# Cross-covariance attention with a gated FFN: norms from running sums, products spread over three chunks, first softmax by blocks, last stores by pairs

## The chip, the cores and the metric

The kernel runs on one core of one Trainium2 chip. The metric is device time in microseconds (us) for one execution: 810.92 us before the change, the median of 3 runs (810.77 to 811.05).

## What is computed

For each of 4 batches, q, k and v have N = 6016 rows and C = 256 columns. The attention is over columns: q and k are divided by the norm of each of their columns, the 256x256 matrix of their products is put through a softmax, and v is multiplied by it. The 24064 rows of the result then pass a gated feed-forward layer of width 1536.

```python
qn = q / (np.linalg.norm(q, axis=1, keepdims=True) + 1e-06)
kn = k / (np.linalg.norm(k, axis=1, keepdims=True) + 1e-06)
s = kn.transpose(0, 2, 1) @ qn / tau
a = np.exp(s - s.max(-1, keepdims=True))
a /= a.sum(-1, keepdims=True) + 1e-09
x = (v @ a).reshape(24064, 256)
gate = 1.0 / (1.0 + np.exp(-(x @ w_gate)))
out = (gate * (x @ w_val)) @ w_out
```

tau is 1. All inputs and the output are float32; the matmuls take bfloat16.

## The kernel before

A batch has 47 row tiles of 128 rows, worked off as 12 chunks (`groups`): eleven of four tiles and one of three. The attention is folded into the feed-forward weights: with e the exponentials, G = e w_gate and H = e w_val, each row divided by its sum of e, are made once a batch, so that a chunk needs only v times G and v times H. G and H come from 12 products (`gh_order`) of two matmuls of 512 columns each.

A chunk has 12 slots, one per block of 128 of the 1536 hidden columns. In a slot `glu` issues two matmuls into `ps_gate` and two into `ps_val`; ScalarE makes a tanh (L516), VectorE combines it with `ps_val` into `hT` (L517). Each of the two PSUM tags has two buffers. The products with w_out belong to the chunk before (`out_work`): per pair of row tiles seven half-size products instead of eight, in Strassen's manner, whose operands VectorE adds up from `hT` (`a_sum`, L539). `run_work` issues in every slot its share of them. When a pair is through, ScalarE copies it out (L593, L600) and GpSimd makes the last additions (L594, L595, L608, L609). SyncE stores whole chunks.

The order of everything is written out by hand: `tc.manual_schedule()` keeps the program's order on each engine. Next to chunks of batch b, `side_work` puts steps for batch n = b+1 at numbered slots, chunk times 12 plus slot. A step is issued at the end of its slot, after `glu`, the sums and the share of output products:

- slots 0 to 95: loads of q and k on GpSimd's queue, two `score` matmuls per row tile, squares by ScalarE and their running sums `acc` in VectorE (`acc_square`, `acc_add`; L278). The last `acc_add` is in slot 96 for batch 1, and in slot 95 for batches 2 and 3.
- slots 97 to 114: `acc_fold`, three steps for q and three for k (L288, L292, L295, L296): four row sums become one in float32, which is split into two bfloat16 parts.
- slot 117: `norms_mm` sums over the partitions with 8 products of one column into `ps_n`. Slot 118: `root_seed` (two VectorE operations) and `root_steps` (13 small GpSimd operations). Slot 124: `norms_inv` (L369, L370). Slot 125: `spread_both` puts k's inverse norms along the columns with float32 matmuls (`ps_rk`). Slot 126: ScalarE copies it. Slot 127: `scale_x` (L308). Slots 128, 129: `exps`. Slot 131: `sums_both`.
- slots 132 to 143: one of the 12 `gh` products each, with alternating PSUM buffers; even ones are evicted by ScalarE (L464), odd ones by VectorE (L466).

Batch 0 has a head of its own: q and k come by DMA in groups (`groups0`), with squares, running sums and scores as they land. `busy` issues idle matmuls between them. Then come a root by ScalarE (`norms_sqrt`), `norms_inv`, copies of the scores (`copy_s`), `spread_k`, `weights` (two products on VectorE per block, then an exponential), the first transposed v, the row sums and four `gh` products; the other eight follow in chunk 0.

The last chunk's output rows have a tail of their own: `end_rows` makes rows 0 and 1 with plain products, `store` stores what is in `stores`, and `last_rows` stores these two rows on SyncE's queue, makes the last row tile in two halves and stores one on SyncE's and one on ScalarE's queue.

## Time and profile before

| what | value |
|---|---|
| median of 3 runs | 810.92 us |
| the profiled execution | 811.63 us |
| its span, first to last instruction | 809.9 us |
| mean granted TensorE clock | 0.997 |
| TensorE busy | 785.4 us (97%) |
| VectorE busy | 719.5 us (89%) |
| ScalarE busy | 525.8 us (65%) |
| GpSimd busy | 351.9 us (43%) |
| first gate product of chunk 0 | 38.03 us |
| last matmul starts | 804.46 us |

Engines in the profile: PE is TensorE's matmul, PEld its weight load, DVE VectorE, ACT ScalarE, POOL GpSimd, SP SyncE; a q behind an engine's name stands for its queue. A timeline line gives the start, the duration, the engine, the line of the kernel, the operation, output<-inputs, the shapes and, in brackets, how long the engine was idle before it and what ended that. Matmuls are pipelined: a product of 512 columns has a duration of 0.38 us, and the next one starts 0.216 us after it. A line of the table of stages gives from:to, the elapsed time, and for each engine its busy time with the number of instructions, then the granted clock, the DMA engines' share and GB/s. Times in a stage count from the start of the span.

### The profile page before, as it was taken

The numbers are of one execution on the slowest core, as the hardware profiler recorded it, in microseconds if no ns is written. First come the engines' busy times: TensorE is split into PE (matmuls) and PEld (weight loads), VectorE is DVE, ScalarE is ACT, GpSimd is POOL, SyncE is SP. The second block draws the span as 40 slices with busy tenths as digits, with TensorE's granted clock in tenths as the row PEclk, the third lists the DMA queues.
The fourth block names the chain that finished last, engine by engine and source line by source line (L and its number), as shares of the span: only waits on it lengthen the run. The fifth ranks groups of instructions, "written<-read, shape, count | busy, mean of one in ns | idle before, by whom it ended". The sixth has DMA issues, their size and how long they took to land.

```text
span 809.9 us, 17873 instructions
## 1 busy us (share of the span) xinstructions
PE 785.4 (97%) x6742; PEld 500.3 (62%) x6754; DVE 719.5 (89%) x1230; ACT 525.8 (65%) x887; POOL 351.9 (43%) x566
## 2 busy tenths in 40 slices
PE   4799999999999999999999999999999999999997
PEld 2556666666666666666666666666666666666665
DVE  5768999999889999999997999999998898998995
ACT  3666777765667777775566677776566566566563
POOL 4572545433543454334543543443353234444343
PEclk9999999999999999999999999999999999999999
DMA  9995757422856557423285477523223433323302
GB/s 214 207 207 96 129 99 139 89 63 47 137 102 122 90 115 126 84 53 78 58 148 105 94 124 111 103 68 78 60 53 74 78 53 80 79 53 85 68 27 74
DMA packets 76775, 78.24 MB, mean 97 GB/s; under 512 B 50704, under 2 KB 54288, under 8 KB 76688
## 3 DMA queue, kind: packets, MB, share of 16 engines
q0 software_dynamic: 21648, 39.59, 29.6%
q1 hardware_dynamic: 54752, 36.91, 20.0%
q8 instruction: 53, 0.87, 0.4%
q10 hardware_dynamic: 288, 0.59, 0.2%
q14 instruction: 34, 0.28, 0.1%
HBM read 78.64 MB, written 24.64 MB: 128 GB/s over the span
## 4 chain that ended last, share of the span: by engine, by line
PE 89%; DVE 5%; DMA 3%; issue 1%; ACT 1%; POOL 0%; POOLq 0%; DVEq 0%
PE ps_gate L127 28%; PE ps_val L127 28%; PE ps_o L127 26%; PE ps_s L127 4%; DMA k_sb<-in_k_dram 3%; DVE hT L517 2%; PE ps_gh L127 2%; DVE sums L539 1%; ACT g_sb L516 1%; DVE fold L295 0%; PE ps_rk L127 0%; DVE two L292 0%; DVE acc L278 0%; POOL q_sb L137 0%; PE ps_end L127 0%
## 5 line engine op out<-in xcount | busy, mean ns | idle before, releaser
L516 ACT ACTIVATE g_sb<-ps_gate 128x512 f32<-128x512 f32 (+1 forms) x576 | 338.3, 588 | 228.5 <-PE ps_gate L127 218.6
L517 DVE SCALAR_TENSOR_TENSOR hT<-g_sb,ps_val 128x512 bf16<-128x512 f32 (+1 forms) x576 | 384.8, 671 | 68.4 <-ACT g_sb L516 59.9
L127 PE MATMUL ps_val<-vT,gh_H 128*128 128x512 bf16 (+1 forms) x1152 | 337.5, 375 | 2.0 <-DVE hT L517 2.0
L127 PE MATMUL ps_gate<-vT,gh_G 128*128 128x512 bf16 (+1 forms) x1152 | 337.5, 375 | 0.4
L539 DVE TENSOR_TENSOR sums<-hT 128x768 bf16<-128x768 bf16 (+1 forms) x460 | 280.4, 610 | 0.0
L127 PEld LDWEIGHTS <-sums 128*128 128x128 bf16 x2670 | 183.1, 98 | 82.2
L127 PEld LDWEIGHTS <-gh_H 128*128 128x128 bf16 x1152 | 112.7, 98 | 133.6 <-issue 3.4
L608 POOL TENSOR_TENSOR out_sb<-out_sb,m_sb 128x256 f32<-128x256 f32 x89 | 76.8, 863 | 244.7 <-ACT out_sb L600 216.2
L127 PE MATMUL ps_o<-w_sums,sums 128*128 128x128 bf16 x1602 | 154.7, 219 | 0.0
L127 PEld LDWEIGHTS <-hT 128*128 128x128 bf16 x1200 | 88.3, 98 | 46.7
L594 POOL TENSOR_TENSOR m_sb<-m_sb 128x128 f32<-128x128 f32 x89 | 41.7, 469 | 155.4 <-ACT m_sb L593 155.3
L127 PEld LDWEIGHTS <-gh_G 128*128 128x128 bf16 x1152 | 96.9, 98 | 15.1 <-DVE gh_G L466 0.5
L127 PE MATMUL ps_o<-w_out_sb,sums 128*128 128x128 bf16 x1068 | 96.2, 219 | 0.0
L127 PE MATMUL ps_o<-w_sums,hT 128*128 128x128 bf16 x1068 | 95.7, 219 | 0.0
L127 PE MATMUL ps_s<-k_sb,q_sb 128*128 128x256 bf16 x376 | 71.4, 293 | 14.5 <-DMA k_sb<-in_k_dram 7.6
L609 POOL TENSOR_TENSOR out_sb<-out_sb 128x256 f32<-128x256 f32 x89 | 77.7, 873 | 7.0
L600 ACT COPY out_sb<-ps_o 128x512 f32<-128x512 f32 x89 | 52.2, 586 | 14.3 <-PE ps_o L127 11.6
L278 DVE TENSOR_TENSOR acc<-acc,sq 128x1024 bf16<-128x1024 bf16 (+1 forms) x66 | 59.8, 906 | 0.0
L595 POOL TENSOR_TENSOR m_sb<-m_sb 128x128 f32<-128x128 f32 x89 | 53.5, 601 | 7.0
L240 ACT ACTIVATE sq<-k_sb 128x1024 bf16<-128x1024 bf16 (+2 forms) x44 | 44.8, 1027 | 11.9 <-DMA k_sb<-in_k_dram 11.9
L127 PEld LDWEIGHTS <-q_sb 128*128 128x128 bf16 x376 | 33.8, 105 | 20.0 <-issue 8.9
L593 ACT COPY m_sb<-ps_o 128x384 f32<-128x384 f32 x89 | 42.7, 479 | 2.6 <-PE ps_o L127 0.3
(82 smaller groups left out, 313.3 us busy)
## 6 DMA issues: line engine op xcount, KB each, us to landing
out_dram<-out_sb SPq DMA_DIRECT2D x44, 512.0 KB, 3.4
v_sb<-in_v_dram POOLq DMA_DIRECT2D x44, 256.0 KB, 5.2
q_sb<-in_q_dram POOLq DMA_DIRECT2D x35, 256.0 KB, 4.4
k_sb<-in_k_dram POOLq DMA_DIRECT2D x35, 256.0 KB, 5.7
q_sb<-in_q_dram POOLq DMA_DIRECT2D x4, 512.0 KB, 11.5
k_sb<-in_k_dram POOLq DMA_DIRECT2D x4, 512.0 KB, 13.4
w_f<-in_moe_w_out_dram POOLq DMA_DIRECT2D x3, 512.0 KB, 10.5
out_dram<-out_sb SPq DMA_DIRECT2D x3, 384.0 KB, 2.8
```

Of the source, the lines that this page charges most:

```text
L127: nc.tensor.matmul(out, lhsT=lhsT, rhs=rhs, start=start, stop=stop, **kw)
L240: nc.scalar.activation(out=sq[:, :nt, :], in_=src[:, :nt, :], func=ACT.Square)
L278: nc.vector.tensor_tensor(out=acc[:, :nt, :], in0=acc[:, :nt, :], in1=st[b]["sq", w][:, :nt, :], op=ALU.add)
L516: nc.scalar.activation(out=g_sb[:, :n], in_=ps_gate[:, :n], func=ACT.Tanh, scale=0.5)
L517: nc.vector.scalar_tensor_tensor(out=hts[b, ci][:, f, :n], in0=g_sb[:, :n], scalar=1.0, in1=ps_val[:, :n], op0=ALU.add, op1=ALU.mult,)
L539: nc.vector.tensor_tensor(out=sums[b, ci, g][:, m, :, : half * P], in0=hT[:, f0 + k0 : f1 : 2, ds(r0 * half * P, half * P)], in1=hT[:, f0 ...
L593: nc.scalar.copy(m, states[p]["ps"][:, : 3 * P].rearrange("p (n c) -> p n c", c=P))
L594: nc.gpsimd.tensor_tensor(out=m[:, 1, :], in0=m[:, 1, :], in1=m[:, 2, :], op=ALU.add)
L595: nc.gpsimd.tensor_tensor(out=m[:, 2, :], in0=m[:, 1, :], in1=m[:, 0, :], op=ALU.add)
L600: nc.scalar.copy(o[:, p : p + half + 1 : half, :], states[p]["ps"].rearrange("p (t c) -> p t c", c=C),)
L608: nc.gpsimd.tensor_tensor(out=ends, in0=ends, in1=states[p]["m"][:, 1:3, :], op=ALU.add)
L609: nc.gpsimd.tensor_tensor(out=ends, in0=ends, in1=mids, op=ALU.subtract)
```

## The change

The fold is gone: `norms_mm` takes the products of the four running sums themselves, 16 instead of 8. All steps from `norms_mm` on move ahead: `norms_mm` to slot 97, `root_seed` and `root_steps` to 98, `norms_inv` to 106, `spread_both` to 107, the copy to 108, `scale_x` to 109 and 110, `exps` to 111 and 112, the row sums to 114. The 12 `gh` products go to slots 116, 118, 121, 123, 126, 128, 131, 133, 136, 138, 141 and 143.

In the head, the last group's scores are issued before the last norm products, the copies of the scores before `norms_inv`, and four short `busy` products become two `busy_long` of float32 after groups 6 and 8; later ones are fewer. `weights` multiplies a block with k's inverse norms in one VectorE operation, and q's go into the exponential as its scale, one ScalarE operation for each 128 columns. The row sums (`row_sums`, for `sums_both`) are made block by block, VectorE alone evicts the first transposed v, and the `gh` evictions change engines.

In the tail, chunk 10 of the last batch is stored by pairs of rows, each when its additions are done; those of its last pair are made by VectorE instead of GpSimd. Its output products are shared over 11 slots of the last chunk instead of 12. Each of the rows of `end_rows` is stored at once on ScalarE's queue.

```diff
--- before.py
+++ after.py
@@ -279,27 +279,10 @@
             out=acc[:, :nt, :], in0=acc[:, :nt, :], in1=st[b]["sq", w][:, :nt, :], op=ALU.add
         )
 
-    def acc_fold(b, w, step):
-
-        s = st[b]
-        if step == 0:
-            acc = s["acc"][w]
-            s["two"] = attp.tile([P, 2, C], FP32, tag="two", name="two")
-            nc.vector.tensor_tensor(out=s["two"], in0=acc[:, :2, :], in1=acc[:, 2:, :], op=ALU.add)
-            return
-        one, other = s["two"][:, 0, :], s["two"][:, 1, :]
-        if step == 1:
-            nc.vector.tensor_tensor(out=one, in0=one, in1=other, op=ALU.add)
-            return
-        fold = attp.tile([P, 2, C], BF16, tag=f"fold{w}", name="fold")
-        nc.vector.tensor_copy(out=fold[:, 0, :], in_=one)
-        nc.vector.tensor_tensor(out=fold[:, 1, :], in0=one, in1=fold[:, 0, :], op=ALU.subtract)
-        s.setdefault("fold", []).append(fold)
-
     def norms_mm(b):
         s = st[b]
         s["n"] = psm.tile([P, 2 * CB], FP32, tag="m", name="ps_n")
-        norm_mms(s["n"], s["fold"], 2, True, True)
+        norm_mms(s["n"], s["acc"], TPC, True, True)
 
     def scale_x(b, j):
         s = st[b]
@@ -391,18 +374,17 @@
         s = st[b]
         e = attp.tile([P, CB, P], BF16, tag=f"e{i}", name=f"e_sb{i}", bufs=2)
         y = attp.tile([P, CB, P], FP32, tag=f"y{i}", name="y_sb")
+        nc.vector.tensor_tensor(
+            out=y,
+            in0=s["x"][:, :, ds(i * P, P)],
+            in1=s["rk"][i].rearrange("p (o c) -> p o c", o=1).to_broadcast([P, CB, P]),
+            op=ALU.mult,
+        )
         for j in range(CB):
-            nc.vector.scalar_tensor_tensor(
-                out=y[:, j, :],
-                in0=s["x"][:, j, ds(i * P, P)],
-                scalar=s["r"][:, j : j + 1],
-                in1=s["rk"][i],
-                op0=ALU.mult,
-                op1=ALU.mult,
-            )
-        nc.scalar.activation(out=e, in_=y, func=ACT.Exp, bias=shift)
+            nc.scalar.activation(
+                out=e[:, j, :], in_=y[:, j, :], func=ACT.Exp, bias=shift, scale=s["r"][:, j : j + 1]
+            )
         s.setdefault("e", []).append(e)
-        s.setdefault("rrow", [])
 
     def exps(b, i):
 
@@ -412,26 +394,27 @@
             out=e, in_=s["x"][:, :, ds(i * P, P)], func=ACT.Exp, bias=shift
         )
         s.setdefault("e", []).append(e)
-        s.setdefault("rrow", [])
-
-    def sums_both(b):
-        s = st[b]
-        ps_r = psm.tile([P, CB], FP32, tag="m", name="ps_r")
-        for i in range(CB):
+
+    def row_sums(b, i0, ni, pl, tag):
+        s = st[b]
+        ps_r = pl.tile([P, ni], FP32, tag=tag, name="ps_r")
+        for i in range(ni):
             for j in range(CB):
                 mm(
                     ps_r[:, i : i + 1],
-                    s["e"][i][:, j, :],
+                    s["e"][i0 + i][:, j, :],
                     ones_bf[:, 0:1],
                     start=(i == 0 and j == 0),
                     stop=(j == CB - 1),
                     skip_group_check=True,
                 )
-        r = attp.tile([P, CB], FP32, tag="rrow", name="rrow", bufs=2)
+        r = attp.tile([P, ni], FP32, tag=f"rrow{i0}", name="rrow", bufs=2)
+        half = attp.tile([P, ni], FP32, tag=f"rhalf{i0}", name="rhalf", bufs=2)
         invert(r, ps_r, 1e-9, 1.0)
-        half = attp.tile([P, CB], FP32, tag="rhalf", name="rhalf", bufs=2)
         nc.vector.tensor_scalar(out=half, in0=r, scalar1=0.5, scalar2=None, op0=ALU.mult)
-        s["rrow"] = [[x[:, i : i + 1] for i in range(CB)] for x in (r, half)]
+        rrow = s.setdefault("rrow", ([], []))
+        for x, to in zip((r, half), rrow):
+            to.extend(x[:, i : i + 1] for i in range(ni))
 
     def gh_tiles(b):
         st[b]["gh"] = [
@@ -605,9 +588,14 @@
             c00, c11 = 2 * p, 2 * (half + p) + 1
             ends = blocks[:, c00 : c11 + 1 : c11 - c00, :]
             mids = blocks[:, c00 + 1 : c11 : max(1, c11 - c00 - 2), :]
-            nc.gpsimd.tensor_tensor(out=ends, in0=ends, in1=states[p]["m"][:, 1:3, :], op=ALU.add)
-            nc.gpsimd.tensor_tensor(out=ends, in0=ends, in1=mids, op=ALU.subtract)
-            if p == half - 1:
+            last = (b, ci) == (B - 1, NCH - 2)
+            add = (nc.vector if last and p == half - 1 else nc.gpsimd).tensor_tensor
+            add(out=ends, in0=ends, in1=states[p]["m"][:, 1:3, :], op=ALU.add)
+            add(out=ends, in0=ends, in1=mids, op=ALU.subtract)
+            if last:
+                t0 = groups[ci][0]
+                nc.sync.dma_start(out=out_rows[b][:, t0 + p : t0 + nt : half, :], in_=o[:, p:nt:half, :])
+            elif p == half - 1:
                 stores.append((b, ci))
 
         def single(s, f):
@@ -652,14 +640,15 @@
         ps = pso.tile([P, CH], FP32, tag="o", name="ps_o")
         for f in range(FC):
             mm(ps[:, :C], hT[:, f, ds(s * P, P)], w_out_sb[:, f, :], f == 0, f == FC - 1)
-        nc.vector.tensor_copy(out=out_tile(b, ci)[:, s, :], in_=ps[:, :C])
+        o = out_tile(b, ci)[:, s, :]
+        nc.vector.tensor_copy(out=o, in_=ps[:, :C])
+        nc.scalar.dma_start(out=out_rows[b][:, groups[ci][0] + s, :], in_=o)
 
     def last_rows(b, ci):
 
         t0, nt = groups[ci]
         s, half = nt - 1, C // 2
         hT = hts[b, ci]
-        nc.sync.dma_start(out=out_rows[b][:, t0 : t0 + s, :], in_=ffn[b, ci][:, :s, :])
         for n, queue in enumerate((nc.sync, nc.scalar)):
             ps = pso.tile([P, half], FP32, tag="o", name="ps_end")
             for f in range(FC):
@@ -674,6 +663,11 @@
         ps = psg.tile([P, CH], FP32, tag="g", name="ps_busy")
         for _ in range(n):
             mm(ps, ones_bf, ones_wide, True, True)
+
+    def busy_long():
+
+        ps = psg.tile([P, CH], FP32, tag="g", name="ps_busy")
+        mm(ps, ident_f, ident_f.rearrange("p (o c) -> p o c", o=1).to_broadcast([P, TPC, P]), True, True)
 
     ps_n0 = psm.tile([P, 2 * CB], FP32, tag="m", name="ps_n")
 
@@ -702,37 +696,34 @@
             ends.append((sq, nt))
         if g == last0:
             norm_mms(ps_n0, acc, TPC, True, False)
+        for u in range(nt):
+            score(0, t0, u)
+        if g == last0:
             for n, (end, rows_n) in enumerate(ends):
                 norm_mms(ps_n0, end, rows_n, False, n == len(ends) - 1, (1, 0) if n else (0, 1))
-        for u in range(nt):
-            score(0, t0, u)
-        if n_acc - 4 <= g < n_acc:
-            busy(1)
+        if g in (6, 8):
+            busy_long()
     st[0]["n"] = ps_n0
     norms_sqrt(0)
     nc.scalar.preload_act_table(ACT.Exp)
-    norms_inv(0)
     copy_s(0, 0)
     copy_s(0, 1)
-    busy(3)
+    norms_inv(0)
+    busy(2)
     spread_k(0, 0, pso, "o")
     spread_k(0, 1, pso, "o")
-    busy(1)
     weights(0, 0)
     weights(0, 1)
-    late = []
-    transpose_v(
-        0, 0, psv.tile([P, TPC * CB, P], BF16, tag="v", name="ps_tp"), lambda *a: late.append(a)
-    )
-    nc.scalar.copy(*late.pop())
+    transpose_v(0, 0, psv.tile([P, TPC * CB, P], BF16, tag="v", name="ps_tp"))
     gh_tiles(0)
 
-    ps_first = gh_mms(0, 0, psg, "g")
-    sums_both(0)
-    gh_store(0, 0, ps_first, False)
-    gh(0, 1, psg, "g", act=True)
-    gh(0, 2, psv, "v", act=False)
-    gh(0, 3, psv, "v", act=True)
+    row_sums(0, 0, 1, psm, "m")
+    gh(0, 0, psg, "g", act=True)
+    row_sums(0, 1, 1, pso, "o")
+    gh(0, 1, psg, "g", act=False)
+    gh(0, 2, psv, "v", act=True)
+    gh(0, 3, psv, "v", act=False)
+
 
     def side_work(b):
 
@@ -776,23 +767,21 @@
         if n + 1 < B:
             for g, (t0, nt) in enumerate(groups[:3]):
                 at(NCH * FC - 24 + 8 * g, load_qk, n + 1, t0, nt)
-        for i in range(6):
-            at(8 * FC + 1 + (7 * i + 1) // 2, acc_fold, n, *divmod(i, 3))
-        s0 = 10 * FC - 3
+        s0 = 8 * FC + 1
         at(s0, norms_mm, n)
         at(s0 + 1, root_seed, n)
         at(s0 + 1, root_steps, n)
-        at(s0 + 7, norms_inv, n)
-        at(s0 + 8, spread_both, n)
-        at(s0 + 9, copy_rk, n)
-        at(s0 + 10, scale_x, n, 0)
-        at(s0 + 10, scale_x, n, 1)
-        at(s0 + 11, exps, n, 0)
-        at(s0 + 12, exps, n, 1)
-        at(s0 + 14, sums_both, n)
-        at(s0 + 14, gh_tiles, n)
+        at(s0 + 9, norms_inv, n)
+        at(s0 + 10, spread_both, n)
+        at(s0 + 11, copy_rk, n)
+        at(s0 + 12, scale_x, n, 0)
+        at(s0 + 13, scale_x, n, 1)
+        at(s0 + 14, exps, n, 0)
+        at(s0 + 15, exps, n, 1)
+        at(s0 + 17, row_sums, n, 0, CB, psm, "m")
+        at(s0 + 17, gh_tiles, n)
         for i in range(len(gh_order)):
-            at(s0 + 15 + i, gh, n, i, *((pss, "s"), (psm, "m"))[i % 2])
+            at(s0 + 19 + 5 * i // 2, gh, n, i, *((pss, "s"), (psm, "m"))[i % 2])
         return side
 
 
@@ -812,7 +801,7 @@
                         store()
                     if f + final in NEXT_SLOTS and prev != (0, 0):
                         a_sum(*prev, 1, NEXT_SLOTS[f + final])
-                    run_work(work, 1 / (FC - f))
+                    run_work(work, 1 / max(1, FC - final - f))
                 if f in OWN_SLOTS and not final and (b, ci) != (0, 0):
                     a_sum(b, ci, 0, OWN_SLOTS[f])
                 for fn, a in side.get((ci, f), ()):
```

## The prediction

> **What bounds the kernel now.** I read the page first, then the table of stages, then TensorE's and VectorE's timelines where a stage is longer than its neighbours, then the head and the tail.
>
> From the page: busy time, and the chain that ended last.
>
> ```profile
> PE 785.4 (97%) x6742; PEld 500.3 (62%) x6754; DVE 719.5 (89%) x1230; ACT 525.8 (65%) x887; POOL 351.9 (43%) x566
> PE 89%; DVE 5%; DMA 3%; issue 1%; ACT 1%; POOL 0%; POOLq 0%; DVEq 0%
> ```
>
> TensorE sets the pace; the 5% DVE in the chain are the places where something else does. The table of stages, one line per chunk: a clean chunk of the last batch, then chunks 8 to 11 of the second (elapsed, then busy time of PE, weight loads, DVE, ACT, POOL).
>
> ```profile
> 742.90:757.96 15.06, 15.06 (x137) 9.40 (x134) 13.60 (x23) 9.14 (x16) 6.28 (x9) 1.00 0.32 71
> 363.89:379.68 15.79, 15.21 (x136) 9.38 (x134) 15.75 (x26) 9.14 (x16) 6.17 (x9) 1.00 0.31 69
> 379.68:394.93 15.25, 15.25 (x144) 9.58 (x142) 15.06 (x28) 9.15 (x16) 5.97 (x9) 1.00 0.27 62
> 394.93:411.11 16.18, 15.86 (x143) 10.01 (x141) 14.21 (x29) 10.09 (x19) 9.88 (x24) 1.00 0.55 98
> 411.11:428.78 17.67, 17.51 (x160) 11.73 (x160) 15.25 (x32) 11.38 (x23) 7.98 (x13) 1.00 0.64 120
> ```
>
> A clean chunk has no TensorE idle, so one slot (one `glu` call with its share of output products) is 15.05/12 = 1.254 us. Chunk 8 is 0.74 longer without more TensorE work, and its DVE is full (15.75 of 15.79). Chunk 11 holds all twelve G and H products: 24 matmuls of 0.216 are 5.18, a three-row chunk is 12.45 (the last of the kernel), the sum 17.63 against 17.67. So the products are not stalled where they are. The two stalls in the timelines of batch 0 (VectorE, then TensorE):
>
> ```profile
> 181.37 1.01 DVE L539 TENSOR_TENSOR sums<-hT 128x768 bf16<-128x768 bf16 x1
> 182.31 0.81 DVE L295 CAST fold<-two 128x256 bf16<-128x256 f32 x1
> 183.15 0.43 DVE L296 TENSOR_TENSOR fold<-two,fold 128x256 bf16<-128x256 f32 x1
> 183.49 0.68 DVE L517 SCALAR_TENSOR_TENSOR hT<-g_sb,ps_val 128x512 bf16<-128x512 f32 x1
> ...
> 183.05 0.59 PE L127 MATMUL ps_gate<-vT,gh_G 128*128 128x512 bf16 x2
> 184.22 0.59 PE L127 MATMUL ps_val<-vT,gh_H 128*128 128x512 bf16 x2 [0.58 <-DVE hT L517]
> 185.04 0.59 PE L127 MATMUL ps_gate<-vT,gh_G 128*128 128x512 bf16 x2
> ...
> 207.49 0.50 PE L127 MATMUL ps_o<-w_out_sb,sums 128*128 128x128 bf16 x6
> 208.36 0.71 PE L127 MATMUL ps_rk<-ident_f,r 128*128 128x128 f32 x4 [0.38 <-DVE r L370]
> ```
>
> The fold makes a gate product late, and TensorE, two buffers ahead, waits: the slot is 1.99 long, 0.74 too long. Then `ps_rk` starts 0.54 late, because `norms_inv` is queued on DVE one slot before it. Both recur in batches 1 and 2 (0.74 and 0.75; 0.49 and 0.62). Some single gaps of 0.219 before products of `ps_gh` are missing records: 38 of the 48 `w_gate` products are in the trace. The tail, SyncE's timeline:
>
> ```profile
> 802.96 0.33 SPq L647 DMA_DIRECT2D out_dram<-out_sb  x1
> 803.82 0.33 SPq L662 DMA_DIRECT2D out_dram<-out_sb  x1
> 804.36 1.52 SPq L669 DMA_DIRECT2D out_dram<-end  x1
> ```
>
> 512, 256 and 64 KB go out within 1.4 us. The two `end` transfers land 4.1 us (SyncE) and 3.3 us (ScalarE, issued at 805.03) after issue, at 808.50 and 808.33; 1.36 us of closing semaphores follow to 809.86.
>
> **What the Trainium skill says.** "TensorE: Matmul & The Clock Gate", *What's actually happening*: after an idle window of about 3.4 us the array runs at half rate until it has been busy for about as long. The trace agrees: products of 256 columns are 0.109 apart at 26.4, 0.213 from 26.7 to 29.7, 0.109 from 30.35. "DMA: Bandwidth & Descriptors", *Anatomy of one DMA*: about 2.0 us fixed plus bytes/436 GB/s; the 384 KB stores give 2.9 by it, 2.8 here. "GPSIMD Engine Reference", *Key points*: GpSimd shares its SBUF interfaces with VectorE when that reads two SBUF inputs; here the same `sums` operation takes 0.55 alone and 1.01 beside L608/L609.
>
> **The change part by part** (us, minus is gain).
>
> *Folds gone.* Six DVE operations a batch, by their rows 2x(0.68+0.67+0.55+0.43) = 4.7 of DVE time. What they cost the end is only the stall: 0.74+0.74+0.75 = -2.23. All else of them lay beside TensorE.
>
> *Norm products on `acc` itself.* 16 instead of 8, at 0.0255 apart (chunk 9's excess of 0.204 over 8): +0.20 a batch, +0.61. Their place is now slot 97, one slot after the last `acc_add` in batch 0 (slot 96), two in batches 1 and 2 (slot 95). In the trace of before that add ends 0.56 after slot 98 begins in batch 0, and 0.35 before it in the others. The first eight products (of q's sums) take 0.20, so the rest wait about 0.41 in batch 0 and nothing else: +0.41. Queued behind them are the gate products of slot 98, which have no other way.
>
> *`root_seed`, `root_steps`, `norms_inv`, `spread_both` earlier.* The 13 GpSimd steps took 4.1 (200.80 to 204.87); ahead of them on POOL is only chunk 7's last addition, and DVE asks for `r` eight slots (10 us) later: hidden. `spread_both` still comes one slot after `norms_inv`. At slot 106 with DVE not late: gate at 376.43 in batch 1, tanh ends at +1.23, hT 0.60, the slot's `sums` 0.47, inverse to first product 0.42 (as at 207.94 to 208.36): 379.21, while TensorE is there at 376.43+2.51 = 378.94. Stall 0.27, against 0.54, 0.49, 0.62: -0.83 over three batches. Bounds: DVE free of waits and no stall, -1.65; as before, 0.
>
> *Products spread.* The same 24 matmuls, evictions and weight loads in slots 116 to 143; nothing was stalled, so 0. The cover is DVE's slack in chunk 9: 15.05-13.60 = 1.45, plus TensorE's new work there 0.10+2x0.43 = 0.96, against DVE's new work 2x0.48 (`scale_x`) + 0.73 (row sums inverted) + 0.74 (one eviction) = 2.43. That just balances, and a gate product may be 1.08 late before TensorE feels it (hT ends 1.86 after its slot's start; the product that reuses its buffer starts at 2.94). Bounds: 0, and all DVE evictions in the four-row slots exposed, which the rivals use.
>
> *Head.* DMA lands the last of k at 32.31 and the first gate weights at 35.91 either way. Moving two score products ahead of the last norm products delays the root 33.04 to 33.19 and brings the copies of s to 32.92 to 33.64; `norms_inv` behind them ends at 33.93 (before 33.63). `ps_rk` to first use 0.64: 34.57. Two DVE operations of 128x256 (0.42, 0.34 apart; L387 takes 0.41, L308 0.48) replace four of 0.34. Four exponentials of 128 columns with two pointer operands: by "ScalarE: Activation LUTs", *What ACT_TABLE_LOAD costs*, 0.186+2x0.093+0.107 = 0.48 each, 0.39 apart, an estimate (the page gives 0.49 for the old form, the trace 0.507). First block ready at 35.90, second at 36.67, instead of 35.42 and 35.94. The first product stays at 36.05, held by its weights; the second waits until 36.80 (before 36.58). Evictions then end at 37.41, 38.19, 38.55, 39.05, and the first gate products run at 38.09 instead of 38.03: +0.06. The late block uses up slack that evictions had. `busy_long` is four `ps_rk`-like products (2x0.112 each), 0.9 warm and 1.8 cold: the second ends at about 29.3, and groups 9 and 10 are through by 31.4, before the k of group 11 lands at 31.61. The dropped and changed `busy` products stand against the clock gate: between 33.4 and 36.8 TensorE would be busy 57% instead of 72%; between 19.8 and 23.2 it was about 55% and the clock held. Bounds: -0.15; +2.0 if the clock falls for one window (half of 3.4, and the late block).
>
> *Tail.* With the output work done in 11 slots, 7.64 products go into a slot instead of 7; slots of 1.042 become 1.078 and slot 10 ends at 799.90. The last pair's two additions go to DVE before the last hT: ScalarE's copy ends at 800.70, two additions of 0.42 (L296's 0.43) to 801.55, hT to 802.05, while row 0's twelfth product wants it at 801.76: TensorE +0.35. In return 256 KB leave at about 799, 256 at 801.6, 128 at 802.9 and 804.2, and the last 64 KB at 805.38 (805.03+0.35) with little ahead. The new issues on ScalarE's queue (0.35 each) have no other work beside them. Fixed part and size give 2.15; I take 2.4 for what still overlaps: lands 807.8 instead of 808.5, so -0.7. Bounds -1.2 (2.0, no stall) and +0.3 (3.3 again).
>
> Sum: -2.23+0.61+0.41-0.83+0.06-0.7 = -2.68. The profiled execution took 811.63, of which 809.86 span and 1.8 around it; it would take 808.95. It lies 0.7 above the median of the runs, 810.92, so the median becomes 808.2.
>
> **The rivals.** *The waits only move* (same): `norms_mm`, `spread_both` and the last hT all wait on DVE by one slot. If `spread_both` gains nothing (+0.83), each batch waits for `acc` (+0.8) and the tail is even (+0.7), 2.3 come back: 810.5. For it, the 0.54 before; against it, the 0.35 margin in batches 1 and 2. *DVE becomes the bound in chunks 9 and 10* (slower): four evictions of 0.74 a batch fall into full slots. If POOL's sharing stretches the operations there, as it did the fold's cast (0.81 against 0.28), and their time shows in full, 4x0.74-1.08 = 1.9 a batch, 5.6 in all: 813.8. It ends on the slow side once over 1.4 a batch shows. For it, the balance of chunk 9; against it, chunk 11, which takes six such evictions without a stall. *More than forecast*: no stall at `ps_rk`, no wait in batch 0, tail -1.2: 806.4. *The clock falls in the head*: +1.9, 810.1, belongs to "same".
>
> **How the numbers follow.** Forecast 0.54 (own range 807.0 to 809.3, by the bounds of head, tail and `ps_rk`); waits move or clock falls 0.24; DVE bound 0.17; more 0.05. 0.2% (1.6 us, about what a measurement of this kernel can tell from no change) puts nearly all of the first case and the last into faster: 0.58; same 0.24; slower 0.18. The range 806.6 to 812.6 leaves out the upper part of the DVE case and a little below.
>
> **What would show it.** Right: no slot of 1.99 at 107; a gap of about 0.4 before `ps_n` in batch 0 alone; `ps_rk` 0.2 to 0.3 late; first gate products within 0.3 of 38.0; last landing about 2.4 after the last issue. Wrong: TensorE waiting for DVE's hT or evictions in chunks 9 or 10, products of 0.43 instead of 0.216 after 36, a last transfer that lands 3 us or more after issue.

## The result and the profile after

The changed kernel takes 808.53 us (median of 6 runs, 808.16 to 808.78) against 811.03 (6 runs of the kernel before, 810.77 to 811.05): a ratio of 0.9969, 95% interval 0.9957 to 0.9982. The forecast was 808.2, range 806.6 to 812.6. The profiled execution took 808.34 us, its span 806.5 (806.48 unrounded) against 809.86: 3.38 less. Read part by part, those 3.38 us come from three places, and one of them, the last chunk with the stores behind it, gave more than twice what was predicted:

| place | before | after | difference | predicted |
|---|---|---|---|---|
| start to the first gate product of chunk 0 | 38.03 | 38.18 | +0.16 | +0.06 |
| chunks 8 to 11, batch 0 | 64.95 | 64.62 | -0.33 | |
| the same, batch 1 | 64.89 | 64.19 | -0.70 | |
| the same, batch 2 | 65.03 | 64.19 | -0.84 | |
| sum of these three | | | -1.87 | -2.04 |
| first gate product of the last chunk to the end | 21.80 | 20.14 | -1.67 | -0.7 |
| span | 809.86 | 806.48 | -3.38 | -2.68 |

Each column is one profiled execution. That of the kernel before (811.63) lies above all six of its timed runs, and the median moved by 2.50 us, less than the span.

The page of the changed kernel, engines' busy time and the chain that ended last:

```profile
PE 785.5 (97%) x6776; PEld 500.1 (62%) x6776; DVE 707.7 (88%) x1209; ACT 526.4 (65%) x888; POOL 356.7 (44%) x564
PE 92%; DMA 3%; DVE 3%; ACT 1%; issue 1%; POOL 0%; DVEq 0%; POOLq 0%
```

TensorE has the same work as before (785.4), VectorE 11.8 us less, and VectorE's share of the chain falls from 5% to 3%. Of the idle time on TensorE, a part is gone. Where the rest lies, the table of stages shows: chunks 8 to 11 of batch 1 of the changed kernel, elapsed time, then busy time of PE, weight loads, DVE, ACT and POOL.

```profile
363.70:380.01 16.31, 16.12 (x155) 10.31 (x153) 15.12 (x29) 9.75 (x17) 10.57 (x22) 1.00 0.31 66
380.01:396.03 16.02, 16.02 (x143) 9.87 (x140) 13.84 (x27) 10.15 (x19) 6.24 (x9) 1.00 0.26 59
396.03:413.24 17.21, 17.21 (x146) 10.37 (x144) 14.72 (x26) 10.55 (x19) 7.27 (x12) 1.00 0.51 92
413.24:427.89 14.65, 14.65 (x144) 10.37 (x143) 12.07 (x25) 9.39 (x20) 8.15 (x13) 1.00 0.83 145
```

Chunks 9 to 11 have no TensorE idle; chunk 8 keeps some, and it holds all the steps from `norms_mm` to `spread_both`. Its two waits, in the timelines of batch 0 of the changed kernel (TensorE, and two VectorE lines among them):

```profile
171.90 0.34 PE L127 MATMUL ps_n<-ones_bf,acc 128*128 128x1 bf16 x8
172.52 0.35 PE L127 MATMUL ps_n<-ones_bf,acc 128*128 128x1 bf16 x8 [0.28 <-DVE acc L278]
172.74 0.59 PE L127 MATMUL ps_gate<-vT,gh_G 128*128 128x512 bf16 x2
...
185.10 0.16 DVE L352 TENSOR_SCALAR r<-r 128x4 f32<-128x4 f32 x1
185.30 0.18 DVE L353 RECIPROCAL r<-r 128x4 f32<-128x4 f32 x1
...
184.89 0.55 PE L127 MATMUL ps_o<-w_sums,sums 128*128 128x128 bf16 x7
185.63 0.68 PE L127 MATMUL ps_rk<-ident_f,r 128*128 128x128 f32 x4 [0.19 <-DVE r L353]
186.15 0.59 PE L127 MATMUL ps_gate<-vT,gh_G 128*128 128x512 bf16 x2
```

The first eight norm products run at 171.90 and take 0.20; the other eight wait for the last `acc_add`. Counted from start to start, 0.415 is lost there, in batch 0 only. `ps_rk` starts 0.35 late in each batch: seven products at 0.0545 from 184.89 end their turn at 185.27, and r is ready at about 185.48. (The bracket shows less because it counts from the modelled end of a product.) No gate or value product waits on `hT` in these chunks any more.

In the tail, TensorE waits once, in row 0: 11 products at 0.109 apart from 798.83 end their turn at 800.03, and the next starts at 800.46, 0.43 late.

```profile
798.83 1.36 PE L127 MATMUL ps_o<-w_out_sb,hT 128*128 128x256 bf16 x11
800.46 1.59 PE L127 MATMUL ps_o<-w_out_sb,hT 128*128 128x256 bf16 x13 [0.27 <-DVE hT L500]
```

At the end of the program the view of the DMA transfers shows which store was how late: the stretch from 800 to 810 us, first of the kernel before. Its GB/s row has 40 slices of 0.25 us; the issue lines end with the size and the time from issue to landing.

```profile
GB/s 0 0 0 0 0 0 0 0 0 0 0 0 0 0 66 360 360 393 377 410 295 385 336 129 199 133 162 33 25 25 20 20 8 0 0 0 0 0 0 0
q8 instruction: 1, 0.02, 1.1%
out_dram<-out_sb SPq DMA_DIRECT2D x1, 512.0 KB, 4.6
out_dram<-out_sb SPq DMA_DIRECT2D x1, 256.0 KB, 4.4
out_dram<-end SPq DMA_DIRECT2D x1, 64.0 KB, 4.1
out_dram<-end ACTq DMA_DIRECT2D x1, 64.0 KB, 3.3
```

And the same stretch of the changed kernel:

```profile
out_dram<-out_sb SPq DMA_DIRECT2D x1, 256.0 KB, 2.2
out_dram<-out_sb ACTq DMA_DIRECT2D x2, 128.0 KB, 2.3
out_dram<-end SPq DMA_DIRECT2D x1, 64.0 KB, 1.6
out_dram<-end ACTq DMA_DIRECT2D x1, 64.0 KB, 1.5
```

The last 64 KB now land 1.55 us after issue, not the 2.4 of the forecast. The rows of before say why I had misread them: from 806.75 to 808.25 only 33 to 8 GB/s move, about a sixteenth of the 393 that sixteen DMA engines moved together at 804.25. The single packets of that stretch follow one another with no other beside them, eight of 2 KB, then eight of 512 B and again eight of 512 B: a sixteenth of the 256 KB store and of each 64 KB store. So it is not a queue of bytes ahead of a small store that all engines work off; the share of one DMA engine is late, alone. And among the packets between 800 and 810 us is one of queue q8, of the kind instruction: a fetch of instructions.

### The profile page after: what moved, and what is told of

Same layout as the page of the kernel before. It is cut to its first block, busy times and chain, and to the rows that moved or that the text cites. A ratio compares the mean times of both kernels' runs of the same rounds, so it can differ in the third digit from the quotient of the medians.

```text
span 806.5 us, 17904 instructions
## 1 busy us (share of the span) xinstructions
PE 785.5 (97%) x6776; PEld 500.1 (62%) x6776; DVE 707.7 (88%) x1209; ACT 526.4 (65%) x888; POOL 356.7 (44%) x564
## 3 DMA queue, kind: packets, MB, share of 16 engines
q1 hardware_dynamic: 55008, 36.64, 20.0%
## 4 chain that ended last, share of the span: by engine, by line
PE 92%; DMA 3%; DVE 3%; ACT 1%; issue 1%; POOL 0%; DVEq 0%; POOLq 0%
PE ps_gate L127 29%; PE ps_val L127 29%; PE ps_o L127 26%; PE ps_s L127 4%; DMA k_sb<-in_k_dram 3%; PE ps_gh L127 2%; DVE hT L500 1%; DVE sums L522 1%; ACT g_sb L499 0%; PE ps_rk L127 0%; DVE acc L278 0%; ACT e_sb L384 0%; PE ps_n L127 0%; POOL q_sb L137 0%; PE ps_end L127 0%
## 5 line engine op out<-in xcount | busy, mean ns | idle before, releaser
L522 DVE TENSOR_TENSOR sums<-hT 128x768 bf16<-128x768 bf16 (+1 forms) x460 | 276.9, 602 | 0.0
L593 POOL TENSOR_TENSOR out_sb<-out_sb,m_sb 128x256 f32<-128x256 f32 x88 | 79.9, 908 | 233.6 <-ACT out_sb L583 205.0
L127 PE MATMUL ps_s<-k_sb,q_sb 128*128 128x256 bf16 x376 | 69.0, 285 | 15.2 <-DMA k_sb<-in_k_dram 8.6
L594 POOL TENSOR_TENSOR out_sb<-out_sb 128x256 f32<-128x256 f32 x88 | 75.3, 856 | 6.9
```

What stands on the lines that cost most here:

```text
L127: nc.tensor.matmul(out, lhsT=lhsT, rhs=rhs, start=start, stop=stop, **kw)
L522: nc.vector.tensor_tensor(out=sums[b, ci, g][:, m, :, : half * P], in0=hT[:, f0 + k0 : f1 : 2, ds(r0 * half * P, half * P)], in1=hT[:, f0 ...
L593: add(out=ends, in0=ends, in1=states[p]["m"][:, 1:3, :], op=ALU.add)
L594: add(out=ends, in0=ends, in1=mids, op=ALU.subtract)
```

## The experiments

"Tail" below is the time from the first gate product of the last chunk to the end of the span. Each kernel was timed beside the kernel before on the same chip; a ratio is to that.

**The fold alone.** From the kernel before, only the folds are taken out; all other steps stay in their slots.

```diff
-        norm_mms(s["n"], s["fold"], 2, True, True)
+        norm_mms(s["n"], s["acc"], TPC, True, True)
...
-        for i in range(6):
-            at(8 * FC + 1 + (7 * i + 1) // 2, acc_fold, n, *divmod(i, 3))
```

> The kernel before without the fold alone: norms_mm takes the four running sums (16 products), still in slot 117; every other step, the twelve products in slots 132 to 143, head and tail as before. My theory (the fold's place in DVE's queue is what cost TensorE time): slot 107 falls from 1.995 to 1.254 in each batch, slot 117 grows from 1.458 to about 1.66, no wait for acc in batch 0, ps_rk as late as before; chunks 8 to 11 of a batch together 0.54 shorter, the span 1.6 us shorter. Rival (it is the earlier and spread placement that brings the body's gain): a stall of about 0.7 turns up in another slot of chunks 8 to 10 and the span is within 0.5 us of before.

Measured: 807.67 us (5 runs, 807.61 to 807.99), ratio 0.9957 (0.9945 to 0.9970), span 805.9. Chunks 8 to 11 take 64.13, 64.13 and 64.39 in the three batches, 2.22 less in sum. The 0.74 at slot 107 is gone, and `ps_rk`, left in slot 125 and expected to be as late as before, is 0.26, 0.26 and 0.52 late instead of 0.54, 0.49 and 0.62. But the tail is 20.00 instead of 21.80 with not a line of it changed: the last four stores land 2.6, 2.5, 2.1 and 1.7 us after issue. So 1.8 of its 4.0 us come from a place that the edit doesn't touch. This one part of the change is not slower than the whole of it: its span is 0.6 shorter, and the intervals of the two ratios overlap.

**The tail alone.** From the kernel before, only the tail edits (stores by pairs, additions on VectorE, 11 slots, rows stored at once on ScalarE's queue).

```diff
+            if last:
+                t0 = groups[ci][0]
+                nc.sync.dma_start(out=out_rows[b][:, t0 + p : t0 + nt : half, :], in_=o[:, p:nt:half, :])
...
-                    run_work(work, 1 / (FC - f))
+                    run_work(work, 1 / max(1, FC - final - f))
```

> The kernel before with the four edits of the tail alone (pair stores, VectorE for the last pair's additions, rows stored one by one on ScalarE's queue, output work in 11 slots). My theory (fewer bytes ahead of the last transfers): the two end transfers land 1.6 us after issue instead of 4.1 and 3.3, the last hT holds TensorE for about 0.43, the span is 1.6 to 1.7 us shorter, all of it after the start of the last chunk. Rival (the landing time in the changed kernel comes from elsewhere, such as less traffic or a different phase of the core): 3 us or more to landing, and the span 0.3 to 0.5 us longer.

Measured: 810.33 us (13 runs, 810.10 to 812.03), ratio 0.9990 (0.9982 to 0.9998), tail 20.63, chunks as before. Less than expected: the row stores took 3.8 and 2.9 us to land, the last two transfers 2.6 and 2.0. An instruction fetch lies at 804.1 us here.

**Moving the fetch and nothing else.** The trace of each kernel has 53 packets (54 with the larger paddings) of 16 KB in queue q8, one per 255 of TensorE's 13,506 recorded instructions (before). The Trainium skill, "Runtime: NRT & Kernel Launch", *Instruction fetch mechanics*, says that an engine's instructions are refilled in 16 KiB blocks of 256 over a DMA queue of the sequencer's own, and calls the cost "mostly hidden". The count agrees. If the fetch is what holds the stores, 48 more entries in TensorE's stream must move it away from them. So the kernel before got 24 products of one column in the head, with their weight loads:

```diff
+        if g == 4:
+            ps = psg.tile([P, CH], FP32, tag="g", name="ps_pad")
+            for _ in range(24):
+                mm(ps[:, 0:1], ones_bf, ones_bf[:, 0:1], True, True)
```

> The kernel before with 24 products of one column, whose results nobody reads, added in the head where TensorE waits for k (after group 4): 48 more entries in TensorE's instruction stream, nothing else. My new theory (the 16 KB packets of the instruction kind on queue 8 are fetches of TensorE's instructions, one for 256 of them; the one at 803.7 runs into the last stores, and the bytes ahead of these are not what makes them late): all chunks as before to 0.05 us, the last fetch about 2.4 us earlier at 801.2 or before, the end transfers land 1.6 to 2.2 us after issue instead of 4.1 and 3.3, the span about 1.8 us shorter. Rival (my prediction's term, 768 KB ahead of the last transfers): nothing changes, span 809.6 to 809.9.

Measured: 810.33 us (21 runs, 810.10 to 811.72), ratio 0.9989 (0.9983 to 0.9996). The first gate product is 0.51 later, every chunk as before, and the tail 20.01 instead of 21.80. The same stretch of its trace:

```profile
GB/s 0 0 0 0 0 0 0 0 0 0 66 0 0 0 0 0 0 344 410 393 393 410 320 401 377 277 279 68 0 0 0 0 0 0 0 0 0 0 33 0
out_dram<-out_sb SPq DMA_DIRECT2D x1, 512.0 KB, 2.6
out_dram<-out_sb SPq DMA_DIRECT2D x1, 256.0 KB, 2.5
out_dram<-end SPq DMA_DIRECT2D x1, 64.0 KB, 2.2
out_dram<-end ACTq DMA_DIRECT2D x1, 64.0 KB, 1.7
```

The fetch is the lone 66 in the slice at 802.5, just ahead of the stores (at 802.64; I had expected 801.2 or before); then the stores move at up to 410 GB/s to the end, and the thin stretch is gone. (The 33 near the end is a fetch of 8 KB in another queue, q14.) Work that does nothing made the tail 1.8 us shorter.

**The old tail in the changed kernel.** The edits of the second experiment, undone.

> The changed kernel with the tail of before (one store of the chunk, additions on GpSimd, rows 0 and 1 in one store, output work in 12 slots). TensorE's instruction stream is as long as the changed kernel's, so the last fetch stays near 801.9 minus 0.3. My new theory (the edits of the tail bring nothing where no fetch falls onto the last stores, and cost the wait for the last hT): from the first gate product of the last chunk to the end 20.0 us against the changed kernel's 20.14, span within 0.3 us of it. Rival (the prediction's: smaller stores land sooner): end transfers 3 us or more after issue and the span 1.0 to 1.7 us longer.

Measured: 808.35 us (5 runs, 808.06 to 808.56), ratio 0.9962 (0.9950 to 0.9975), tail 20.25 against 20.14, all else as in the changed kernel. So 1.55 of the 1.67 that the tail gained would have come without the tail edits. Where no fetch meets the stores they gain nothing: the old tail took 20.00 and 20.01 in the two experiments above (the fold alone and the 24 products), the new one 20.14.

**Moving the fetch back.** The changed kernel with 3 times 39 one-column products more in its head, so that the fetch falls later.

```diff
+        if g in (0, 2, 4):
+            ps = psg.tile([P, CH], FP32, tag="g", name="ps_pad")
+            for _ in range(39):
+                mm(ps[:, 0:1], ones_bf, ones_bf[:, 0:1], True, True)
```

> The changed kernel with 117 one-column products more in the head (39 after each of groups 0, 2 and 4), 234 entries more in TensorE's instruction stream, so that the blocks of 256 entries end 22 entries later in the tail. If a store is held back by a fetch of TensorE's instructions: the last fetch moves from 801.9 to about 803.1 (plus what the head shifts), onto the two end transfers, which then land 2.5 us or more after issue instead of 1.55, and first gate of the last chunk to end grows from 20.14 to 20.7 or more; all else as in the changed kernel. Rival, that the place of the fetch is of no account: landing 1.5 to 1.7 after issue and 20.1 to 20.2, and the span as the changed kernel's but for what the head shifts.

Measured: 809.25 us (9 runs, 808.98 to 809.77), ratio 0.9975 (0.9965 to 0.9984), span 807.3, of which the head is 0.68 later. The fetch came at 802.98, and it met the two row stores (3.4 and 2.6 us to landing instead of 2.8 and 1.8) more than the last two transfers (2.2 and 1.7 instead of 1.6 and 1.5). The tail is 20.27, only 0.13 longer. The direction is the fetch theory's, the size is not what I expected of it: with stores of 128 and 64 KB apart from each other most of the delay was over when the last transfer went out.

The old tail and the late fetch together in the changed kernel (3 times 37 products):

> The changed kernel with the old tail, and 111 one-column products more in the head, so that TensorE's last instruction fetch moves back from 63 entries ahead of its end (800.7) to some 30 ahead, which is where the kernel before has it (29 ahead, at 803.74). If the tail edits gain only by being less exposed to a fetch: the stores at the end take 3.5 to 4.6 us to land as in the kernel before, and first gate of the last chunk to end is 21.3 to 21.9 instead of 20.25, span about 808.4 to 809.0 with 0.7 of it from the longer head. Rival, that the 21.80 of the kernel before came from elsewhere: 20.2 to 20.5 as with the new tail and the late fetch (20.27), span about 807.4.

Measured: 810.35 us (12 runs, 809.70 to 811.03), ratio 0.9987 (0.9979 to 0.9996), span 809.2, tail 21.75. The span is 0.2 over what I expected; 0.36 of it lies in batch 2, where `ps_rk` came 0.71 late instead of 0.35. From the view of the DMA transfers, 800 to 810:

```profile
GB/s 0 0 0 0 0 0 0 0 0 0 0 0 180 360 426 344 426 336 344 369 262 191 133 232 35 16 25 25 18 14 0 0 0 0 0 0 0 0 0 0
out_dram<-out_sb SPq DMA_DIRECT2D x1, 512.0 KB, 4.5
out_dram<-out_sb SPq DMA_DIRECT2D x1, 256.0 KB, 4.3
out_dram<-end SPq DMA_DIRECT2D x1, 64.0 KB, 4.1
out_dram<-end ACTq DMA_DIRECT2D x1, 64.0 KB, 3.2
```

The thin stretch of the kernel before is back, with the same run of single packets, and so are its landing times to 0.1 us. All kernels of this question together, from the packets of queue q8 and the stores' landings (us; "left" counts TensorE's recorded instructions after the fetch began; the last stores are 512, 256, 64 and 64 KB with the old tail, 128, 128, 64 and 64 KB with the edits):

```
kernel         tail edits  last fetch  lasted  left  last stores, issue to landing   tail
before         no          803.74      1.73    29    4.6  4.4  4.1  3.3              21.80
pad_old_tail   no          803.06      1.73    33    4.5  4.3  4.1  3.2              21.75
old_tail       no          800.74      1.31    63    3.1  2.9  2.2  2.0              20.25
pad_before     no          802.64      0.96    69    2.6  2.5  2.2  1.7              20.01
fold_out       no          800.03      0.96    67    2.6  2.5  2.1  1.7              20.00
tail_only      yes         804.08      1.48    33    3.8  2.9  2.6  2.0              20.63
pad_after      yes         802.98      1.23    35    3.4  2.6  2.2  1.7              20.27
after          yes         801.87      0.96    51    2.8  1.8  1.6  1.5              20.14
```

With some 30 entries left the fetch costs the old tail 1.5 to 1.8 us and the new one 0.1 to 0.5; with 50 or more left the two tails are within 0.25 of each other. What the tail edits bring is that a fetch hurts less.

These tails are one execution each, and those of `before` and `pad_old_tail` are among the longer ones of their kernels. By the medians, with the longer heads taken off, the late fetch costs the old tail 1.6 us (`before` against `pad_before`, on one chip). Through the ratios, which is rougher, it is about 1.3 for `pad_old_tail` against `old_tail`, and the edits are worth about 0.9 under a late fetch (`pad_old_tail` against `pad_after`). Timed beside each other, the 34 runs of the kernel before spread from 810.67 to 811.89, while 19 of the 21 of the padded one lie between 810.10 and 810.56; that the fetch's delay differs from execution to execution fits this, but is not shown.

**The spread undone.** The changed kernel with its 12 G and H products in slots 132 to 143.

```diff
-            at(s0 + 19 + 5 * i // 2, gh, n, i, *((pss, "s"), (psm, "m"))[i % 2])
+            at(s0 + 35 + i, gh, n, i, *((pss, "s"), (psm, "m"))[i % 2])
```

> The changed kernel with the twelve G and H products back in slots 132 to 143, one a slot; all else as changed. My theory (spreading is worth nothing, since nothing was stalled where they were): chunks 8 to 11 of a batch together within 0.05 us of the changed kernel's 64.19 in batch 1, the span within 0.2 us. Rival (spreading keeps ScalarE and VectorE from falling behind): chunk 11 shows waits of ps_gate or ps_val for evictions, and the span is 0.6 us or more longer.

Measured: 808.89 us (6 runs, 808.43 to 809.55), ratio 0.9971 (0.9959 to 0.9982). The sums of chunks 8 to 11 are 64.62 and 64.19 in batches 0 and 1, the same as with the spread, and 64.55 in batch 2, where `ps_rk` once came 0.72 late; `pad_old_tail`, which has the spread, shows the same there, so this lateness also comes with the spread. Spreading moves time from chunk 11 (17.67 to 14.65) into chunks 9 and 10 and changes no sum.

**The first softmax in its old form**, in the changed kernel (two VectorE products per block, each with q's and k's norms, and one exponential per block).

> The changed kernel with the old form of the first softmax (four VectorE products with both norms, one exponential of 256 columns a block); order, row sums and evictions as changed. My theory (four exponentials with two pointer operands at 0.385 apart bring the second block 0.7 late, which is what moved the head by 0.16): second block ready at about 36.35 instead of 36.80, first gate product at 37.9 to 38.0 instead of 38.18. Rival (the head is held by the copies of s ahead of norms_inv, or by the weights' DMA): 38.1 to 38.2 again.

Measured: 808.02 us (4 runs, 807.99 to 808.05), ratio 0.9959 (0.9945 to 0.9972), first gate product at 37.88 instead of 38.18. First the changed kernel's head (VectorE, ScalarE, then TensorE):

```profile
34.69 0.75 DVE L377 TENSOR_TENSOR y_sb<-x_sb,ps_rk 128x256 f32<-128x256 f32 x2 [0.58 <-PE ps_rk L127]
35.15 1.65 ACT L384 ACTIVATE e_sb<-y_sb,shift,r 128x128 bf16<-128x128 f32 x4 [0.49 <-DVE y_sb L377]
36.89 0.59 PE L127 MATMUL ps_gh<-w_gate,e_sb 128*128 128x512 bf16 x2
38.18 0.59 PE L127 MATMUL ps_gate<-vT,gh_G 128*128 128x512 bf16 x2
```

and that of the old form:

```profile
34.80 1.13 DVE L378 SCALAR_TENSOR_TENSOR y_sb<-x_sb,r,ps_rk 128x128 f32<-128x128 f32 x4 [0.58 <-PE ps_rk L127]
...
36.59 0.59 PE L127 MATMUL ps_gh<-w_gate,e_sb 128*128 128x512 bf16 x2
37.88 0.66 PE L127 MATMUL ps_gate<-vT,gh_G 128*128 128x512 bf16 x2
```

VectorE takes 0.38 less in the new form, but the four exponentials need 1.65 us in a row, and the second block's products start at 36.89 instead of 36.59. Made of 128 columns at a time, the exponentials of the first softmax cost 0.3 us.

**No idle products.** The changed kernel without both `busy_long` and without `busy(2)`.

> The changed kernel without any idle products in the head (neither busy_long nor busy). My theory (they matter only for TensorE's clock, which must be up when the first G and H products run at 36): if the clock falls, products of 512 columns are 0.43 apart from 36 on until TensorE has been busy for one window, first gate product near 40 and the span 1.5 to 2.5 us longer; that is my expectation, since TensorE would be busy for only about 45% of 33.4 to 36.8. Rival (the scores keep the clock up by themselves): 0.216 apart, span within 0.1 us.

Measured: 809.83 us (13 runs, 808.24 to 811.12), ratio 0.9980 (0.9972 to 0.9987), first gate product at 39.63, 1.45 later. Two windows of its trace, then one of the changed kernel's (the last three numbers: granted clock, DMA share, GB/s):

```profile
33.60:37.00 3.40, 1.78 (x16) 1.31 (x17) 2.41 (x9) 2.87 (x5) 1.66 (x3) 0.94 1.24 205
37.10:39.60 2.50, 2.50 (x8) 0.88 (x8) 1.23 (x4) 1.27 (x2) 1.51 (x3) 0.50 1.24 205
...
33.60:37.00 3.40, 2.12 (x20) 1.44 (x20) 2.32 (x9) 2.91 (x6) 1.70 (x3) 1.00 1.24 206
```

Without the idle products the clock falls to 0.50 at 36.57 and stays there for 3.41 us; in the second window the G and H products are 0.427 apart. The first window, 52% busy (1.78 of 3.40), reaches into that; of the 3.41 us just before the fall, TensorE was busy for 51%. In the changed kernel the window from 33.6 to 37.0 is 62% busy and the clock stays at 1.00. So the rival of the falling clock was real, and it is the idle products, the float32 and the late ones together, that held it off in the changed kernel. Whether the clock falls in every run without them is open: these 13 runs spread over 2.9 us, the six of the changed kernel over 0.6.

**Without the waits of one slot.** The changed kernel's three waits that are left, taken apart: `norms_mm` one slot later in batch 0, the root one slot later, `spread_both` and what follows it one slot later, and VectorE's last two additions after the last `hT`.

```diff
-        at(s0, norms_mm, n)
-        at(s0 + 1, root_seed, n)
-        at(s0 + 1, root_steps, n)
+        at(s0 + (1 if b == 0 else 0), norms_mm, n)
+        at(s0 + 2, root_seed, n)
+        at(s0 + 2, root_steps, n)
...
-        at(s0 + 10, spread_both, n)
+        at(s0 + 11, spread_both, n)
...
+            if last and p == half - 1:
+                deferred.append(finish)
...
+    for finish in deferred:
+        finish()
```

> The changed kernel with its three one-slot waits taken apart: norms_mm and the root one slot later in batch 0 (root one later in all), spread_both and all after it one slot further from norms_inv, products in slots 117 to 143, and VectorE's additions for the last pair issued behind the last hT. My theory (each wait is one step on TensorE queued too close behind its source on VectorE): the gap before ps_n in batch 0 (0.41), those before ps_rk (3 times 0.35) and that in row 0 of the tail (0.43) go, the span is 1.9 us shorter than the changed kernel's, about 804.6. Rival (VectorE is simply full there, and the wait turns up at the next step): under 0.5 us shorter, with gaps before ps_val or ps_gh in chunks 8 to 10.

Measured: 806.49 us (5 runs, 806.38 to 806.64), ratio 0.9942 (0.9929 to 0.9954), span 804.6. Chunks 8 and 9 of batch 1:

```profile
363.03:378.48 15.45, 15.45 (x152) 9.78 (x150) 14.27 (x26) 9.15 (x16) 9.84 (x22) 1.00 0.32 70
378.48:394.99 16.51, 16.51 (x147) 10.37 (x145) 14.89 (x29) 10.85 (x21) 6.10 (x9) 1.00 0.25 57
```

Elapsed and TensorE's busy time are equal in both; all three batches have 63.82 in chunks 8 to 11, and the tail is 19.67. With the old form of the first softmax on top:

> The version without one-slot waits (better), and in the head the old form of the first softmax (two products on VectorE per block, one exponential per block). If the new form costs 0.3 us in the head on its own, as old_weights said: first gate product at about 38.0 instead of 38.31, nothing else changed, span about 804.3, median about 806.2 (better 806.49). Rival: with the other head steps as they are in better, something else holds the first gate (the gate weights or evictions): first gate 38.2 or later and span 804.6 or more.

Measured: 806.07 us (5 runs, 805.96 to 806.22), ratio 0.9934 (0.9922 to 0.9947), span 804.2, first gate product at 37.84, chunks and tail as in the version without it. It beats both kernels.

## Why the prediction was right, and where it was not

Direction and time were right: 808.2 forecast, 808.53 measured. By its own steps:

- *Folds gone*, -2.23: right in place. No gate product waits on the fold, and taking it out alone shortened chunks 8 to 11 by 2.22, with 0.61 more norm products and 0.61 less wait at `ps_rk` in that sum. With its span 0.6 below the changed kernel's, nothing that these runs show came from the rest of the change but a tail less exposed to a fetch.
- *Norm products on `acc` itself*, +0.61 and +0.41: right within 0.02. Slot 97 takes 2.09 in batch 0 and 1.66 in the others, against 1.254 and 0.40 of products, and the wait is in batch 0 alone.
- *`spread_both` earlier*: 0.35 late instead of 0.27 (the terms as written add up to 379.15, which would be 0.21). By the lengths of the slots it gives -0.68, not -0.83, and the reason given was wrong. Nearly all of it, 0.61, came in the kernel where only the folds were gone and no step had moved. There the first operation of `norms_inv` begins 1.08 to 1.09 after the start of `spread_both`'s slot, in the changed kernel 1.08, and in the kernel before 1.19 to 1.37: the folds had put VectorE behind, and the other slot brought nothing.
- *Products spread*, 0: right, shown by undoing it. The rival in which VectorE becomes the bound in chunks 9 and 10 has nothing for it: both have no TensorE idle.
- *Head*, +0.06: was +0.16. The first operation of `norms_inv` took 0.32 instead of 0.16 and the inverse was there at 34.11, not 33.93; the second block followed at 36.80, not 36.67. In the run with the spread undone, whose head is the same, that operation took 0.16, the second block was ready at 36.64 and the first gate product ran at 38.03; so the 0.16 is not what the new order costs. That the block form as such was a loss of 0.3 the forecast did not see, since it compared with a second product at 36.58 and not with what the old form would do beside the new order. The clock held, as argued.
- *Tail*, -0.7: this is the step that failed: "I take 2.4 for what still overlaps: lands 807.8 instead of 808.5, so -0.7." The gain was 1.67, and its reason was another. I put the 4.1 and 3.3 us of before down to the bytes ahead of the last 64 KB. With the same stores in the same order and the same tail, but TensorE's instruction fetch 40 entries earlier, they land in 2.2 and 1.7. That the change's own count of instructions moved the fetch from 29 to 51 entries ahead of the end, and with it most of the 1.67 came, is luck. The `hT` stall was sized about right: 0.43 instead of 0.35.
- *From span to median*: the profiled execution of before lay 0.7 above its median, and I subtracted that; the one after lies 0.2 below its own. The span was forecast 0.7 too long, the median 0.3 too short. The time came out well by luck: these two errors have opposite signs.

The rival *the waits only move* holds in part. Three places wait by one slot now: 0.415 once, 0.35 three times, 0.43 in the tail, 1.90 in sum. Taking them apart gave 1.88 of span, with a head 0.13 later in the sum.

Open: why a fetch takes 0.96 us in one kernel and 1.73 in another; whether it takes longer because it shares an engine with the stores, or the stores because of it, these runs don't separate. While the old tail meets the late fetch, SyncE's own issue of its last store takes 1.52 and 1.42 us (`before`, `pad_old_tail`) instead of the 0.33 of `pad_before` and `fold_out`. That one DMA engine alone was late is read from the GB/s rows and from the sizes of the late packets; the packets' engine is not in the trace. The medians of before and after lie 2.5 apart and the profiled spans 3.4; one profile each can't say in which part of the kernel that difference lies.

## What to carry to other kernels

When a store at the very end lands late, look for an instruction fetch among the packets before blaming the bytes ahead of it. Where the fetches fell here depended on how many instructions TensorE had before, so an edit in the head could win or lose 1.3 to 1.8 us in the tail, and a gain that appears there must be tested with padding before it is credited to the edit. Small stores issued apart, as each is ready, lost less to it here than one large store at the end. When a hand-written order puts a step one slot behind what it reads, count whether the slot is enough on the reader's engine with its usual lateness: here three such waits cost as much as the change had gained in the chunks.

## What the hardware showed that was not expected

- TensorE's instructions come in as 16 KB packets, one per some 255 recorded instructions, 0.88 to 1.85 us each in the kernel before. There, 9 of the 11 stores that took over 3.6 us to land have such a fetch between their issue and their landing, while only 4 of the 39 faster ones do; the 384 and 512 KB stores otherwise mostly land in 2.8 and 3.4 us, these 512 KB ones in 4.0 to 5.1. Two late ones (issued at 414.2 and 595.6) have no fetch beside them, so it is not the only thing that holds a store back.
- An undisturbed 64 KB store from ScalarE's queue landed 1.55 us after issue, 256 KB from SyncE's in 2.15. "DMA: Bandwidth & Descriptors", *Anatomy of one DMA*, whose 2.0 us fixed part I had used, gives that fit for software-generated transfers, GpSimd's; for these stores the measurement decides.
- The 128x4 operation of VectorE that begins `norms_inv` took 0.16 to 0.17 us in 41 of its 52 executions in the 13 traces, and 0.28 to 0.42 in the other 11. In each of these 11 it ended within 0.03 us of the end of a GpSimd instruction: a DMA issue in the head, an addition (L595) in batch 2. So it waited for GpSimd, it seems; no run takes the two apart.
